# A feed-forward kernel's first microseconds: tile 0 centred by two sums, the bias turned by VectorE, one group of transposes moved

## The chip, the core and the metric

The kernel runs on one core of a Trainium2 chip. The core has five engines that run side by side, each with its own instruction queue: TensorE (PE; its weight loads are listed as PEld), VectorE (DVE), ScalarE (ACT), GpSimd (POOL) and SyncE (SP), which here does nothing but issue DMAs and wait. They wait for each other only where the program says so, on semaphores. The metric is the device time of one execution in microseconds (us), the median of several runs. The core is alone on the chip in these runs.

## The reference

x is 2048 x 1024, w1 is 1024 x 3584, w2 is 3584 x 1024, all bf16. Each row of x is normalized (mean and variance over its 1024 values), multiplied by w1, a bias b1 is added, the approximate GELU is taken, and the result is multiplied by w2 with a bias b2.

```
y = _layernorm(x, axis=-1)
h = _gelu(jnp.einsum("bsd,df->bsf", y, w1) + b1)
return jnp.einsum("bsf,fd->bsd", h, w2) + b2
```

## The kernel before

**Tiling.** The 2048 rows of x are 16 tiles of 128 rows (one row in each partition), and four tiles make a block of 512 rows. For each block the kernel needs the normalized rows transposed (`yT_sb`: the 1024 features in 8 pieces of 128 partitions, 512 rows along), so that the first product gives h transposed (`hT_sb`: 28 rows of 128 hidden features, 512 along). For each of the 28 rows, 8 matmuls of 128x512 add up in one PSUM bank (L416), ACT reads the bank and writes GELU with the bias as a column per partition (L433), and the second product (L467) reads `hT_sb`. There are eight PSUM banks: one for transposes (`ps_t`), five for the first product (`ps_1`), two for the second (`ps_2`).

**The first block.** All data must come from memory, so block 0 starts in small pieces. The first seven hidden rows are computed in a "wave" of cells of 128x128, one cell for each tile, hidden row and feature piece (dt), in an order written out by hand (`order`, L509 to L524). Into it the transposes on PE of tiles 0 to 3 (`pe_T`, L360) are put at fixed places: `T_PUTS` (L24) says after how many cells a group of transposes comes. Tile 0 is transposed in three groups of pieces (`GROUPS_0`: 0-1, 2-4, 5-7), tiles 1 to 3 in two of four. The first two groups of tile 0 come ahead of all cells, the third at place 14. Each group goes to a PSUM bank, and ACT copies it to `yT_sb` (L383); a group that uses the same bank waits for the copy of the group before. Groups 0 and 2 of tile 0 and all groups of tiles 1 to 3 use the bank `ps_t`. From the eighth hidden row on the rows are computed whole, with 128x512 matmuls; each takes a PSUM bank whose GELU must be done.

**Normalizing tile 0.** PE cannot start before something is centred. For tile 0 only the mean is taken first, and the reciprocal deviation is put in later. Before the change the mean is got in two ways at once: ACT sums the left 512 columns (L495), DVE takes the statistics of the right 512 (`bn_stats`, L261, whose output holds the means of even and odd columns), and one small operation on DVE adds the three numbers to four times the mean (`op_mean0`, L272). Then DVE writes 4x - 4m for tile 0 to a spare buffer (L278), in two pieces, columns 0-255 and 256-1023. Tile 1 is also only centred (L283); tiles 2 and 3 are normalized whole (L287), for which POOL raises the variance to the power -1/2 (L265). For tiles 0 and 1 the factor is applied after the first product: DVE spreads the reciprocal deviations of the 256 rows over all partitions (`ops_rbc`: L322 and sixteen 32x32 transposes, L330) and multiplies each accumulated bank by them (`dve_scale`, L426) before GELU. The factor of tile 0 is 0.25 of its reciprocal deviation there, since 4x - 4m was written.

**Bias.** b1 is loaded as 28 rows of 128 (`b1r_sb`), but GELU needs it as 28 columns of one value per partition. PE transposes it together with tile 2's second group (`with_b1`, L365 to L369, `B1_AT`), into the same bank, and ACT casts it to `b1_sb` (L387). Every GELU waits for that.

**Warm-up.** Ahead of real work PE runs matmuls on constants (L491): 34 without a wait, then 3 that wait for tile 0's mean (`WARM_A`, L21), and 3 after tile 0's second group.

**Queues.** SP issues most loads in the order of `SP_FIRST_LOADS` (L33): tile 0's left half, six chunks of w1 (one feature piece for seven hidden rows each, 224 KB), tile 2's halves, b1, two more chunks, tile 3's halves, then w8, a chunk of 1 MB for the next hidden rows; the rest of w1, block 1 of x, w2, b2 and the other blocks follow. ACT issues tile 0's right half and tile 1. DVE's order in the head is a list (`head`, L500), followed by the spreading of the deviations. After the first wave DVE's work is laid out by a planner (L571 to L586) that mixes work with due times (scaling, output) with filling work (normalizing and transposing the next block).

Of the kernel before, what the change touches and what calls it, by code (L numbers as in the profile page):

```python
# [17 lines left out]
NB2 = 2  # L18
NOB = 2
TAIL_PIECES = 4  # L20
WARM_A = ((34, None), (3, "m4"))  # L21
WARM_B = 3
N_CENTRED = 2
T_PUTS = {0: (None, None, 14), 1: (21, 35), 2: (96, 118), 3: (140, 156)}  # L24
NORM = {0: (0, 2, 8), 1: (0, 4, 8), 2: (0, 4, 8)}
GROUPS_0 = (0, 2, 5, 8)
WAVE_ROWS_0 = 6
WAVE_K = (0, 2, 4, 5, 6, 8)
B1_AT = (2, 1)
GROUPS_1 = (0, 4, 8)  # L30
W1_CHUNK_COLS = (512, 512, 1024, 640)
N_W2_CHUNKS = 4
SP_FIRST_LOADS = ("x0a", "w0", "w1", "w2", "w3", "w4", "w5", "x2a", "x2b", "b1", "w6", "w7", "x3a", "x3b", "w8")  # L33
ACT_FIRST_LOADS = ("x0b", "x1")

T_PE_START = 5.7
# [55 lines left out]
def bass_standalone__mixer_channel_mlp__prompt_kernel(  # L92
# [53 lines left out]
    with ExitStack() as es:  # L146
# [7 lines left out]
        hT_sb = sb("hT_sb", [P, FT, TB], BF16)  # L154
        o_sb = sb("o_sb", [P, NOB, D], BF16)
        b2_sb = sb("b2_sb", [P, D], BF16)
        b1r_sb = sb("b1r_sb", [FT, P], BF16)
        b1_sb = sb("b1_sb", [P, FT], F32)
        ident = sb("ident", [P, P], BF16)
        ones = sb("ones", [P, P], BF16)  # L160
# [1 line left out]
        st_sb = sb("st_sb", [P, NT, 15], F32)  # L162
        mv_sb = sb("mv_sb", [P, NT, 2], F32)
        rstd_sb = sb("rstd_sb", [P, NT], F32)
        half_sb = sb("half_sb", [P, 1], F32)
        m4_sb = sb("m4_sb", [P, 1], F32)
        rq_sb = sb("rq_sb", [P, N_CENTRED, 32], F32)
        rbc_sb = sb("rbc_sb", [P, N_CENTRED, P], F32)

# [16 lines left out]
        x_ev = {}  # L186
        w1_issued = set()

        def dma(dst, src, sig, nbytes):
            dma_q[0].op(lambda e, dst=dst, src=src: e.dma_start(dst, src), sig=sig, sem="d_" + sig, inc=16)  # L190
            dma_bytes[0] += nbytes
            est[sig] = DMA_T0 + dma_bytes[0] / DMA_BYTES_PER_US

# [19 lines left out]
        def issue(item):  # L213
            if item[0] == "x" and item[-1] in "ab":
                i, h = int(item[1:-1]), "ab".index(item[-1])
                dma(x_sb[:, i, h * HC:(h + 1) * HC], xf[i * P:(i + 1) * P, h * HC:(h + 1) * HC], f"x{i}_{h}",
                    P * HC * 2)
                x_ev[i] = (f"x{i}_0", f"x{i}_1")
            elif item == "b1":
                dma(b1r_sb[:, :], b1.rearrange("(t p) -> t p", p=P), "b1", F * 2)  # L220
            elif item[0] == "x":
                load_x_tile(int(item[1:]))
            elif item[0] == "w" and int(item[1:]) < len(w1_chunks):
                load_w1(int(item[1:]))
# [7 lines left out]
        for i in range(TPB):  # L232
            if i not in x_ev:
                load_x_tile(i)
            else:
                for h, evn in enumerate(x_ev[i]):
                    if evn not in est:
                        issue(f"x{i}" + "ab"[h])
        if "b1" not in est:
            issue("b1")  # L240
        for ci in range(len(w1_chunks)):
            if ci not in w1_issued:
# [11 lines left out]
                                          compare_op=ALU.is_equal, fill=0.0, base=0, channel_multiplier=1),  # L254
                waits=["ones"], sig="ident")
        pool.op(lambda e: e.memset(nhalf[:, :], -0.5), sig="nhalf")
        pool.op(lambda e: e.memset(st_sb[:, :, 12:14], 0.0))
        pool.op(lambda e: e.memset(st_sb[:, :, 14:15], LN_EPS * D), sig="eps")

        def op_stats(i, h):  # L260
            return (lambda e, i=i, h=h: e.bn_stats(st_sb[:, i, 6 * h:6 * (h + 1)], x_sb[:, i, h * HC:(h + 1) * HC]),  # L261
# [7 lines left out]
                    [f"st{i}_0", f"st{i}_1", "eps"], f"mv{i}", 0.33)  # L269

        def op_mean0():
            return (lambda e: e.tensor_scalar(out=m4_sb[:, :], in0=st_sb[:, 0, 7:8], scalar1=st_sb[:, 0, 10:11],  # L272
                                              scalar2=half_sb[:, :], op0=ALU.add, op1=ALU.add),
                    ["st0_1", "half"], "m4", 0.1)

        def op_norm(i, c0, c1, sig):
            if i == 0:
                return (lambda e, c0=c0, c1=c1: e.tensor_scalar(  # L278
                            out=o_sb[:, 0, c0:c1], in0=x_sb[:, 0, c0:c1], scalar1=4.0,
                            scalar2=m4_sb[:, :], op0=ALU.mult, op1=ALU.subtract),  # L280
                        ["m4"], sig, 0.02 + (c1 - c0) * 0.00055)
            if i < N_CENTRED:
                return (lambda e, i=i, c0=c0, c1=c1: e.tensor_scalar(  # L283
                            out=x_sb[:, i, c0:c1], in0=x_sb[:, i, c0:c1], scalar1=mv_sb[:, i, 0:1],
                            scalar2=None, op0=ALU.subtract),
                        [f"mv{i}"], sig, 0.02 + (c1 - c0) * 0.00055)
            return (lambda e, i=i, c0=c0, c1=c1: e.tensor_scalar(  # L287
                        out=x_sb[:, i, c0:c1], in0=x_sb[:, i, c0:c1], scalar1=mv_sb[:, i, 0:1],
                        scalar2=rstd_sb[:, i:i + 1], op0=ALU.subtract, op1=ALU.mult),
                    [f"rstd{i}", f"mv{i}"], sig, 0.02 + (c1 - c0) * 0.00055)  # L290
# [12 lines left out]
        def ln_seq(tiles, between):  # L303
# [12 lines left out]
                    seq += ops_norm(i)  # L316
            return seq

        def ops_rbc():
            res = []  # L320
            for i in range(N_CENTRED):
                res.append((lambda e, i=i: e.tensor_scalar(out=rq_sb[:, i, :], in0=ones[:, 0:32],  # L322
                                                           scalar1=rstd_sb[:, i:i + 1], scalar2=(1.0 if i else 0.25),
                                                           op0=ALU.mult, op1=ALU.mult),
                            ["ones", f"rstd{i}"], f"rq{i}", 0.1))
            for tq in range(4):
                for q in range(4):
                    src = rq_sb[32 * tq:32 * (tq + 1), :, :]
                    dst = rbc_sb[32 * q:32 * (q + 1), :, 32 * tq:32 * (tq + 1)]
                    res.append((lambda e, src=src, dst=dst: e.transpose(out=dst, in_=src), [f"rq{N_CENTRED - 1}"],  # L330
                                ("rbc" if tq == 3 and q == 3 else None), 0.1))
            return res
# [24 lines left out]
        bank_read = {}  # L357
        t_banks = [("t", ps_t[:, 0, :]), ("2_0", ps_2b[:, 0, :]), ("t", ps_t[:, 0, :])]

        def pe_T(i, groups, k, with_b1=False):  # L360
            blk, t = divmod(i, TPB)
            j0, j1 = groups[k], groups[k + 1]
            bname, bap = t_banks[k if i == 0 else 0]
            evs = yT_ev.setdefault(i, [None] * DT)
            if with_b1:  # L365
                o = (j1 - j0) * P
                b1t = bap[:, o:o + FT]
                pe.op(lambda e: e.transpose(out=b1t, in_=b1r_sb[:, :], identity=ident[0:FT, 0:FT]),  # L368
                      waits=["ident", "b1"] + ([bank_read[bname]] if bname in bank_read else []))  # L369
            for j in range(j0, j1):  # L370
                waits = []
                if j == j0:
                    waits = ["ident"] + ([bank_read[bname]] if bname in bank_read else [])
                if j == j0 or y_ev[i][j] != y_ev[i][j - 1]:
                    waits.append(y_ev[i][j])
                pe.op(lambda e, i=i, j=j, o=(j - j0) * P, bap=bap: e.transpose(  # L376
                    out=bap[:, o:o + P], in_=(x_sb[:, i] if i else o_sb[:, 0])[:, j * P:(j + 1) * P],
                    identity=ident[:, :]),
                    waits=waits, sig=(f"tp{i}_{k}" if j == j1 - 1 else None))
                evs[j] = f"te{i}_{k}"  # L380
            src = bap[:, 0:(j1 - j0) * P].rearrange("p (j s) -> p j s", j=j1 - j0)
            dst = yT_sb[:, blk % 2, j0:j1, t * P:(t + 1) * P]
            act.op(lambda e, dst=dst, src=src: e.copy(out=dst, in_=src), waits=[f"tp{i}_{k}"], sig=f"te{i}_{k}")  # L383
            bank_read[bname] = f"te{i}_{k}"
            if with_b1:
                bank_read[bname] = "b1c"
                act.op(lambda e: e.copy(out=b1_sb[:, :], in_=b1t), waits=[f"tp{i}_{k}"], sig="b1c")  # L387
            pe_t[0] += (j1 - j0) * 0.056

        crit = []  # L390
# [98 lines left out]
        def warm(n, gate=None):  # L489
            for _ in range(n):  # L490
# [1 line left out]
                                         start=True, stop=True), waits=[gate] if gate else [])  # L492

        act.op(lambda e: e.preload_act_table(ACT.Gelu_apprx_tanh))
        act.op(lambda e: e.activation(out=o_sb[:, 1, 0:HC], in_=x_sb[:, 0, 0:HC], func=ACT.Copy, scale=2.0 / HC,  # L495
                                      accum_out=half_sb[:, :]), waits=[x_ev[0][0]], sig="half")
        for n, gate in WARM_A:
            warm(n, gate)
        dve.op(None, waits=["eps"])
        head = [op_stats(0, 1), op_mean0()] + ops_norm(0) + ln_seq([1], ()) + [op_stats(0, 0), op_aggr(0)]  # L500
        for o in head + ln_seq(list(range(2, TPB)), ()) + ops_rbc():
            dve_put(o)

        for k in range(2):
# [19 lines left out]
            order.insert(n, ("T", t, k))  # L524
        for c in order:
            if c[0] == "T":
                pe_T(c[1], GROUPS_1 if c[1] else GROUPS_0, c[2], with_b1=(c[1:] == B1_AT))
# [102 lines left out]
```

## Time and profile before

| | us |
|---|---|
| median of 3 runs (398.64 to 398.94) | 398.64 |
| the profiled execution | 398.81 |
| its span | 397.5 |
| PE busy | 394.0 |
| DVE busy | 152.8 |
| ACT busy | 83.0 |
| first cell of the wave starts | 5.98 |
| tile 1's first transposes start | 7.66 |
| first matmul of the eighth hidden row starts | 20.64 |

All times of the profile count from the start of the span. Duration and idle time are given for each instruction or group; "idle before" names what ended the wait. The chain that ended last follows the work backward from the end, from each instruction to what released it. A matmul's shown duration (0.22 us for 128 columns) includes its way through the array; matmuls overlap, and in a full stretch of the wave they start 0.056 us apart (61 cells in 3.41 us of the chain).

### The profile page before, as it was taken

The page shows a single profiled execution, that of the slowest core. Times are in us where ns is not written, and L with a number is a line of the kernel's source. Part 1 is how long each engine was busy: PE and PEld are TensorE (multiplying, and loading weights), DVE is VectorE, ACT ScalarE, POOL GpSimd, SP SyncE. Part 2 cuts the span into 40 slices and gives each one's busy share as a digit, 9 for nine tenths or more (in the row PEclk, how much of TensorE's full clock was granted, in tenths as well). Part 3 has the DMA queues.
Part 4 walks back from the last instruction along what each step waited for, and adds up shares of the span by engine and source line. Part 5 has one row for each costly group of instructions (what it writes and reads, how often), then busy time and mean ns, then how long its engine had stood idle before and what let it go on. Part 6 is the DMA issues. An engine that isn't in the chain of part 4 may idle for free.

```text
span 397.5 us, 4880 instructions
## 1 busy us (share of the span) xinstructions
PE 394.0 (99%) x2117; PEld 191.4 (48%) x2117; DVE 152.8 (38%) x341; ACT 83.0 (21%) x125; POOL 9.8 (2%) x25
## 2 busy tenths in 40 slices
PE   8999999999999999999999999999999999999998
PEld 7954444444444444444444444444444444444447
DVE  5837899989999005988100000001100000001011
ACT  4364330000134432000024434100003334400000
POOL 2101000020001000000000000000000000000000
DMA  8999930000000000000000000000000000000000
GB/s 288 359 378 386 387 136 13 26 29 13 27 2 0 2 0 0 29 13 26 28 13 0 2 0 2 11 16 28 13 26 15 0 0 2 0 13 28 13 28 26
DMA packets 16798, 23.64 MB, mean 59 GB/s; under 512 B 1546, under 2 KB 10378, under 8 KB 16778
## 3 DMA queue, kind: packets, MB, share of 16 engines
q1 hardware_dynamic: 16490, 22.95, 16.4%
q10 hardware_dynamic: 288, 0.39, 0.3%
q8 instruction: 16, 0.26, 0.3%
q14 instruction: 4, 0.03, 0.0%
HBM read 19.14 MB, written 4.19 MB: 59 GB/s over the span
## 4 chain that ended last, share of the span: by engine, by line
PE 98%; DMA 1%; DVE 0%; ACT 0%; issue 0%; DVEq 0%
PE ps L467 49%; PE ps L416 41%; PE ps_t L416 8%; DMA x_sb<-in_x_dram 1%; PE ps_t L376 1%; DVE st_sb L261 0%; PE ps L491 0%; ACT yT_sb L383 0%; PE ps L376 0%; DVE o_sb L478 0%; DVE m_sb L272 0%; PE ps_t L368 0%; DVEq L79 0%
## 5 line engine op out<-in xcount | busy, mean ns | idle before, releaser
L467 PE MATMUL ps<-w_sb,hT_sb 128*128 128x512 bf16 (+1 forms) x980 | 194.2, 361 | 0.0
L416 PE MATMUL ps<-yT_sb,w_sb 128*128 128x512 bf16 (+1 forms) x920 | 167.3, 340 | 0.1
L467 PEld LDWEIGHTS ps<-w_sb,hT_sb 128*128 128x128 bf16 x980 | 91.3, 98 | 102.6
L416 PEld LDWEIGHTS ps<-yT_sb,w_sb 128*128 128x128 bf16 x920 | 80.9, 98 | 82.3 <-issue 0.2
L433 ACT ACTIVATE hT_sb<-ps,b_sb 128x512 bf16<-128x512 f32 x94 | 63.9, 688 | 236.6 <-PE ps L416 217.1
L478 DVE TENSOR_TENSOR o_sb<-ps,b_sb 128x512 bf16<-128x512 f32 (+1 forms) x35 | 22.6, 646 | 198.2 <-PE ps L467 198.1
L348 DVE STREAM_TRANSPOSE yT_sb<-x_sb 32x256 bf16<-32x256 bf16 x192 | 83.7, 436 | 26.6 <-PE ps_t L416 23.5
L416 PE MATMUL ps_t<-yT_sb,w_sb 128*128 128x512 bf16 x144 | 34.0, 379 | 0.0
L261 DVE BATCH_NORM_STATS2 st_sb<-x_sb 128x6 f32<-128x512 bf16 x32 | 21.1, 673 | 4.3 <-DMA x_sb<-in_x_dram 4.2
L416 PEld LDWEIGHTS ps_t<-yT_sb,w_sb 128*128 128x128 bf16 x144 | 14.1, 98 | 16.7
L433 ACT ACTIVATE hT_sb<-ps_t,b_sb 128x512 bf16<-128x512 f32 x18 | 12.4, 689 | 17.4 <-PE ps_t L416 14.5
L426 DVE TENSOR_TENSOR ps<-ps,rbc_sb 128x256 f32<-128x256 f32 x24 | 9.7, 428 | 7.0 <-PE ps L416 6.7
L265 POOL TENSOR_TENSOR rstd_sb<-mv_sb,nhalf 128x1 f32<-128x1 f32 x16 | 8.9, 559 | 119.2 <-DVE mv_sb L268 119.2
L287 DVE TENSOR_SCALAR x_sb<-x_sb,mv_sb,rstd_sb 128x1024 bf16<-128x1024 bf16 (+1 forms) x15 | 7.8, 525 | 3.9 <-POOL rstd_sb L265 3.3
L383 ACT COPY yT_sb<-ps_t 128x512 bf16<-128x512 bf16 (+2 forms) x8 | 4.4, 545 | 8.6 <-PE ps_t L376 8.6
L491 PE MATMUL ps<-const-bfloat16-1.0 128*128 128x128 bf16 x40 | 4.0, 278 | 1.4 <-PEq L615 0.8
L491 PEld LDWEIGHTS ps<-const-bfloat16-1.0 128*128 128x128 bf16 x40 | 3.6, 129 | 1.5 <-issue 0.8
L268 DVE BATCH_NORM_AGGREGATE mv_sb<-st_sb 128x2 f32<-128x15 f32 x16 | 3.5, 221 | 1.3
L330 DVE STREAM_TRANSPOSE rbc_sb<-rq_sb 32x64 f32<-32x64 f32 x16 | 3.8, 236 | 0.2
L376 PE MATMUL ps_t<-ident,x_sb 128*128 128x128 bf16 x24 | 2.4, 220 | 0.2 <-ACT yT_sb L383 0.2
L426 DVE TENSOR_TENSOR ps_t<-ps_t,rbc_sb 128x256 f32<-128x256 f32 x4 | 1.6, 410 | 1.7 <-PE ps_t L416 1.7
L376 PEld LDWEIGHTS ps_t<-ident,x_sb 128*128 128x128 bf16 x24 | 1.5, 98 | 0.4 <-ACT yT_sb L383 0.4
(24 smaller groups left out, 7.6 us busy)
## 6 DMA issues: line engine op xcount, KB each, us to landing
w_sb<-in_w_dram SPq DMA_DIRECT2D x4, 1792.0 KB, 18.1
out_dram<-o_sb SPq DMA_DIRECT2D x31, 128.0 KB, 1.7
x_sb<-in_x_dram SPq DMA_DIRECT2D x3, 1024.0 KB, 14.0
w_sb<-in_w_dram SPq DMA_DIRECT2D x2, 1024.0 KB, 9.6
w_sb<-in_w_dram SPq DMA_DIRECT2D x1, 2048.0 KB, 15.1
w_sb<-in_w_dram SPq DMA_DIRECT2D x8, 224.0 KB, 4.2
w_sb<-in_w_dram SPq DMA_DIRECT2D x1, 1280.0 KB, 15.4
x_sb<-in_x_dram SPq DMA_DIRECT2D x5, 128.0 KB, 4.2
```

The lines of the kernel that those rows point to most:

```text
L261: return (lambda e, i=i, h=h: e.bn_stats(st_sb[:, i, 6 * h:6 * (h + 1)], x_sb[:, i, h * HC:(h + 1) * HC]), [x_ev[i][h]], f"st{i}_{h}", 0.65)
L265: pool.op(lambda e, i=i: e.tensor_tensor(out=rstd_sb[:, i:i + 1], in0=mv_sb[:, i, 1:2], in1=nhalf[:, i:i + 1], op=ALU.pow), waits=[f"mv{i} ...
L287: return (lambda e, i=i, c0=c0, c1=c1: e.tensor_scalar(out=x_sb[:, i, c0:c1], in0=x_sb[:, i, c0:c1], scalar1=mv_sb[:, i, 0:1], scalar2=rst ...
L348: res.append((lambda e, src=src, dst=dst: e.transpose(out=dst, in_=src), waits, (f"tr{i}" if lastop else None), 0.47))
L376: pe.op(lambda e, i=i, j=j, o=(j - j0) * P, bap=bap: e.transpose(out=bap[:, o:o + P], in_=(x_sb[:, i] if i else o_sb[:, 0])[:, j * P:(j + ...
L383: act.op(lambda e, dst=dst, src=src: e.copy(out=dst, in_=src), waits=[f"tp{i}_{k}"], sig=f"te{i}_{k}")
L416: pe.op(lambda e, b=b, r=r, dt=dt, n0=n0, n1=n1, bank=bank: e.matmul(unit_bank(bank)[:, n0:n1], lhsT=w1_sb[:, dt, r * P:(r + 1) * P], rhs= ...
L426: crit.append((est[wait_ev], (lambda e, ap=ap: e.tensor_tensor(out=ap, in0=ap, in1=rbc_sb[:, :, :].rearrange("p t s -> p (t s)"), op=ALU.m ...
L433: act.op(lambda e, r=r, n0=n0, n1=n1, bank=bank: e.activation(out=hT_sb[:, r, n0:n1], in_=unit_bank(bank)[:, n0:n1], func=ACT.Gelu_apprx_tanh,
L467: pe.op(lambda e, st=st, ft=ft, c0=c0, c1=c1, bank=bank: e.matmul(ps_2[:, bank, 0:c1 - c0], lhsT=hT_sb[:, ft, st * P:(st + 1) * P], rhs=w2 ...
L478: crit.append((est[sig], (lambda e, ob=ob, c0=c0, c1=c1, bank=bank: e.tensor_tensor(out=o_sb[:, ob, c0:c1], in0=ps_2[:, bank, 0:c1 - c0], ...
L491: pe.op(lambda e: e.matmul(ps_1[:, 0, 0:P], lhsT=unit, rhs=unit, start=True, stop=True), waits=[gate] if gate else [])
```

## The change

Six things are edited together.

1. Tile 0's sums: ACT sums the right half scaled by 1/1024 (event `mean_1`), DVE the left half with a `tensor_scalar` that also gives a sum (event `mean_0`). Each sum is one column of `m_sb`. Nothing adds them: the centring subtracts one column and then the other, and writes x - m instead of 4x - 4m. The factor 0.25 is gone.
2. Tile 0's statistics, formerly the first of DVE's work (right half) and behind tile 1 (left half and aggregate), come behind tile 2's aggregate (left half) and behind tile 3's (right half and aggregate).
3. The bias: four loads of 28 rows of 32 values go to the four groups of 32 partitions of a zeroed buffer, one DVE transpose in 32x32 blocks turns all four, and a DVE copy casts to fp32. These two come on DVE after the head and ahead of the spreading of the deviations. The transpose on PE and the cast on ACT are gone. The loads come behind tile 3's halves instead of ahead of the seventh chunk of w1, and each waits for the zeroing.
4. The third group of tile 0's transposes comes after 6 cells instead of 14.
5. Warm-up: 32 matmuls instead of 34, then 2 instead of 3, which wait for ACT's sum.
6. Two small memsets move from POOL to DVE, and POOL gets the zeroing of the bias buffer.

```diff
-WARM_A = ((34, None), (3, "m4"))
+WARM_A = ((32, None), (2, "mean_1"))
-T_PUTS = {0: (None, None, 14), 1: (21, 35), 2: (96, 118), 3: (140, 156)}
+T_PUTS = {0: (None, None, 6), 1: (21, 35), 2: (96, 118), 3: (140, 156)}
-B1_AT = (2, 1)
-SP_FIRST_LOADS = ("x0a", "w0", "w1", "w2", "w3", "w4", "w5", "x2a", "x2b", "b1", "w6", "w7", "x3a", "x3b", "w8")
+SP_FIRST_LOADS = ("x0a", "w0", "w1", "w2", "w3", "w4", "w5", "x2a", "x2b", "w6", "w7", "x3a", "x3b", "b1", "w8")
...
-                dma(b1r_sb[:, :], b1.rearrange("(t p) -> t p", p=P), "b1", F * 2)
+                b1v = b1.rearrange("(t q a) -> q t a", q=4, a=32)
+                for q in range(4):
+                    dma(b1r_sb[32 * q:32 * q + FT, :], b1v[q], f"b1{q}", F // 2, waits=["b1z"])
...
-        pool.op(lambda e: e.memset(st_sb[:, :, 12:14], 0.0))
-        pool.op(lambda e: e.memset(st_sb[:, :, 14:15], LN_EPS * D), sig="eps")
+        pool.op(lambda e: e.memset(b1r_sb[:, :], 0.0), sig="b1z")
+        dve.op(lambda e: e.memset(st_sb[:, :, 12:14], 0.0))
+        dve.op(lambda e: e.memset(st_sb[:, :, 14:15], LN_EPS * D), sig="eps")
...
         def op_mean0():
-            return (lambda e: e.tensor_scalar(out=m4_sb[:, :], in0=st_sb[:, 0, 7:8], scalar1=st_sb[:, 0, 10:11],
-                                              scalar2=half_sb[:, :], op0=ALU.add, op1=ALU.add),
-                    ["st0_1", "half"], "m4", 0.1)
+            return (lambda e: e.tensor_scalar(out=o_sb[:, 1, HC:D], in0=x_sb[:, 0, 0:HC], scalar1=1.0 / D, scalar2=None,
+                                              op0=ALU.mult, op1=ALU.add, accum_out=m_sb[:, 0:1]),
+                    [x_ev[0][0]], "mean_0", 0.7)
...
-                            out=o_sb[:, 0, c0:c1], in0=x_sb[:, 0, c0:c1], scalar1=4.0,
-                            scalar2=m4_sb[:, :], op0=ALU.mult, op1=ALU.subtract),
-                        ["m4"], sig, 0.02 + (c1 - c0) * 0.00055)
+                            out=o_sb[:, 0, c0:c1], in0=x_sb[:, 0, c0:c1], scalar1=m_sb[:, 0:1],
+                            scalar2=m_sb[:, 1:2], op0=ALU.subtract, op1=ALU.subtract),
+                        ["mean_0", "mean_1"], sig, 0.02 + (c1 - c0) * 0.00055)
...
+        def ops_b1():
+            return [(lambda e: e.transpose(out=b1t_sb[:, :], in_=b1r_sb[:, :]), [f"b1{q}" for q in range(4)], "b1t", 0.2),
+                    (lambda e: e.tensor_copy(b1_sb[:, :], b1t_sb[:, 0:FT]), ["b1t"], "b1c", 0.1)]
...
-        act.op(lambda e: e.activation(out=o_sb[:, 1, 0:HC], in_=x_sb[:, 0, 0:HC], func=ACT.Copy, scale=2.0 / HC,
-                                      accum_out=half_sb[:, :]), waits=[x_ev[0][0]], sig="half")
+        act.op(lambda e: e.activation(out=o_sb[:, 1, 0:HC], in_=x_sb[:, 0, HC:D], func=ACT.Copy, scale=1.0 / D,
+                                      accum_out=m_sb[:, 1:2]), waits=[x_ev[0][1]], sig="mean_1")
...
-        dve.op(None, waits=["eps"])
-        head = [op_stats(0, 1), op_mean0()] + ops_norm(0) + ln_seq([1], ()) + [op_stats(0, 0), op_aggr(0)]
-        for o in head + ln_seq(list(range(2, TPB)), ()) + ops_rbc():
+        head = [op_mean0()] + ops_norm(0) + ln_seq([1], ())
+        mid = {2: lambda: [op_stats(0, 0)], 3: lambda: [op_stats(0, 1), op_aggr(0)]}
+        for i in range(2, TPB):
+            head += [op_stats(i, 0), op_stats(i, 1), op_aggr(i)] + mid[i]() + ops_norm(i)
+        for o in head + ops_b1() + ops_rbc():
             dve_put(o)
```

In `pe_T` the lines under `with_b1` (L365 to L369 and L385 to L387) are taken out.

More of the change, by code (lines that the diff above doesn't have):

```diff
@@ L156, in bass_standalone__mixer_channel_mlp__prompt_kernel @@
         b2_sb = sb("b2_sb", [P, D], BF16)
-        b1r_sb = sb("b1r_sb", [FT, P], BF16)
+        b1r_sb = sb("b1r_sb", [P, 32], BF16)
+        b1t_sb = sb("b1t_sb", [P, 32], BF16)
         b1_sb = sb("b1_sb", [P, FT], F32)
@@ L164, in bass_standalone__mixer_channel_mlp__prompt_kernel @@
         rstd_sb = sb("rstd_sb", [P, NT], F32)
-        half_sb = sb("half_sb", [P, 1], F32)
-        m4_sb = sb("m4_sb", [P, 1], F32)
+        m_sb = sb("m_sb", [P, 2], F32)
         rq_sb = sb("rq_sb", [P, N_CENTRED, 32], F32)
@@ L187, in bass_standalone__mixer_channel_mlp__prompt_kernel, with dma @@
         w1_issued = set()
-        def dma(dst, src, sig, nbytes):
-            dma_q[0].op(lambda e, dst=dst, src=src: e.dma_start(dst, src), sig=sig, sem="d_" + sig, inc=16)
+        def dma(dst, src, sig, nbytes, waits=()):
+            dma_q[0].op(lambda e, dst=dst, src=src: e.dma_start(dst, src), waits=waits, sig=sig, sem="d_" + sig, inc=16)
             dma_bytes[0] += nbytes
@@ L238, in bass_standalone__mixer_channel_mlp__prompt_kernel @@
                         issue(f"x{i}" + "ab"[h])
-        if "b1" not in est:
+        if "b10" not in est:
             issue("b1")
@@ L322, in ops_rbc @@
                 res.append((lambda e, i=i: e.tensor_scalar(out=rq_sb[:, i, :], in0=ones[:, 0:32],
-                                                           scalar1=rstd_sb[:, i:i + 1], scalar2=(1.0 if i else 0.25),
-                                                           op0=ALU.mult, op1=ALU.mult),
+                                                           scalar1=rstd_sb[:, i:i + 1], scalar2=None, op0=ALU.mult),
                             ["ones", f"rstd{i}"], f"rq{i}", 0.1))
@@ L358, in bass_standalone__mixer_channel_mlp__prompt_kernel, with pe_T @@
         t_banks = [("t", ps_t[:, 0, :]), ("2_0", ps_2b[:, 0, :]), ("t", ps_t[:, 0, :])]
-        def pe_T(i, groups, k, with_b1=False):
+        def pe_T(i, groups, k):
             blk, t = divmod(i, TPB)
@@ L364, in pe_T @@
             evs = yT_ev.setdefault(i, [None] * DT)
[L365 to L369, printed above, removed]
             for j in range(j0, j1):
@@ L384, in pe_T @@
             bank_read[bname] = f"te{i}_{k}"
-            if with_b1:
-                bank_read[bname] = "b1c"
-                act.op(lambda e: e.copy(out=b1_sb[:, :], in_=b1t), waits=[f"tp{i}_{k}"], sig="b1c")
             pe_t[0] += (j1 - j0) * 0.056
@@ L526, in bass_standalone__mixer_channel_mlp__prompt_kernel @@
             if c[0] == "T":
-                pe_T(c[1], GROUPS_1 if c[1] else GROUPS_0, c[2], with_b1=(c[1:] == B1_AT))
+                pe_T(c[1], GROUPS_1 if c[1] else GROUPS_0, c[2])
             else:
```

## The prediction

> **What bounds the kernel now.** I read the totals first, then the chain that ended last, then the first 23 us of the timeline, then the landing times of the loads there.
>
> ```profile
> PE 394.0 (99%) x2117; PEld 191.4 (48%) x2117; DVE 152.8 (38%) x341; ACT 83.0 (21%) x125; POOL 9.8 (2%) x25
> ...
> PE 98%; DMA 1%; DVE 0%; ACT 0%; issue 0%; DVEq 0%
> ```
>
> TensorE (PE) is the bound, and the chain leaves it only at the start. So this change can give only what PE still waits for, or does needlessly, in the head. The chain in order of time shows that part:
>
> ```profile
> 0.78 2.80 DMA x_sb<-in_x_dram
> ...
> 6.92 0.18 PE ps_t L376 x3
> 7.10 0.02 issue
> 7.13 0.49 ACT yT_sb L383
> 7.61 0.05 issue
> 7.66 0.40 PE ps_t L376 x4
> ...
> 13.99 0.12 PE ps_t L368
> ```
>
> There are three places: from the landing of tile 0's right half (0.78 + 2.80 = 3.58) to the first transpose; the stay on ACT at 7.13, where PE waits for a copy of tile 0's third group; and the bias transpose (L368). From 7.66 to the end PE has no gap of over 0.1 us but the one at L368. The timeline gives the lines that price the change:
>
> ```profile
> 3.43 0.63 ACT L495 ACTIVATE o_sb<-x_sb 128x512 bf16<-128x512 bf16 x1 [0.45 <-DMA x_sb<-in_x_dram]
> 3.96 0.19 ACT L495 ACTIVATION_READ_ACCUMULATOR o_sb<-x_sb 128x1 f32 x1
> 4.72 0.29 DVE L278 TENSOR_SCALAR o_sb<-x_sb,m_sb 128x256 bf16<-128x256 bf16 x1
> 4.92 0.41 DVE L278 TENSOR_SCALAR o_sb<-x_sb,m_sb 128x768 bf16<-128x768 bf16 x1
> 5.25 0.69 DVE L261 BATCH_NORM_STATS2 st_sb<-x_sb 128x6 f32<-128x512 bf16 x1
> 5.98 0.94 PE L416 MATMUL ps<-yT_sb,w_sb 128*128 128x128 bf16 x14
> 6.89 0.35 DVE L283 TENSOR_SCALAR x_sb<-x_sb,mv_sb 128x512 bf16<-128x512 bf16 x1
> 11.11 0.41 DVE L287 TENSOR_SCALAR x_sb<-x_sb,mv_sb,rstd_sb 128x512 bf16<-128x512 bf16 x1
> 14.57 3.98 DVE L330 STREAM_TRANSPOSE rbc_sb<-rq_sb 32x64 f32<-32x64 f32 x16
> 18.83 2.44 DVE L426 TENSOR_TENSOR ps<-ps,rbc_sb 128x256 f32<-128x256 f32 x7 [0.27 <-PE ps L416]
> ```
>
> Columns are start, duration, engine and line; in brackets the idle time before.
>
> **Step 1, the centre of tile 0.** Before, by the same chain, DVE takes statistics of the right half (3.68 to 4.38), combines them (4.41 to 4.69) and subtracts from 4.72. Now ACT sums the right half while DVE sums the left. ACT's pair took 3.43 to 4.15, 0.72. Started at 3.68, where DVE got the right half, it ends at 4.40; a handover cost 0.04 to 0.06 in the rows (ACT to PE 7.61 to 7.66), so the subtraction starts at 4.45, not 4.72. DVE's sum has no row. The nearest are a 512-wide subtraction without a sum (0.35) and one 512-wide statistics pass plus a one-column operation (0.69 + 0.27 = 0.96); from 3.43 it ends between 3.78 and 4.39, hidden by ACT's 4.40 at both ends. Without that cover (a sum of 1.2 us) the excess of 0.2 would eat most of the gain. The subtraction now reads two columns instead of one: L287 with two took 0.41 for 512 columns, L283 with one 0.35, so 0.06 more for each of two pieces. The first piece ends at 4.45 + 0.29 + 0.06 = 4.80 instead of 5.01: 0.21 sooner. The second starts 0.26 after the first and takes 0.47, so it ends at 5.18 instead of 5.33. Transposes, copy and the first cell follow the first piece: 5.98 becomes 5.77. Bounds: 0.28 if ACT wakes 0.04 after the landing as it did for the left half; 0.05 if ACT loses 0.16 to anything.
>
> **Step 2, the third group sooner.** PE's seven cells before tile 1's first transposes start at 6.93 and end at 6.93 + 7 x 0.056 = 7.32; the transposes start at 7.66. So 0.34 is a wait for the third group's copy. With that group after 6 cells instead of 14, it starts at 5.77 + 6 x 0.056 = 6.10; from first transpose to free bank took 0.90 (6.76 to 7.66), so the copy is done at 7.00. PE arrives at 7.32 - 0.21 = 7.11: that wait is gone. Late next is tile 1's normalization. Its first statistics start at 5.25 now; its load (ACT's second, issued at about 1.24, 3.9 us to landing) comes in at 5.1 to 5.2, so they cannot move by the full 0.15. I take 5.20. From there to the end of the first L283 piece is 6.89 + 0.35 - 5.25 = 1.99, so 7.19, and 0.06 to PE: 7.25. Steps 1 and 2 together bring 7.66 to 7.25, 0.41. Bounds: 0.36 (statistics not sooner than 5.25) and 0.55 (PE's own 7.11). A weight chunk could be late instead:
>
> ```profile
> w_sb<-in_w_dram SPq DMA_DIRECT2D x2, 224.0 KB, 4.3
> x_sb<-in_x_dram SPq DMA_DIRECT2D x1, 128.0 KB, 4.4
> ```
>
> (the loads by issue, the first line in the stretch 3.0 to 3.3, the second in 4.0 to 4.2). The fifth chunk is issued at about 3.1 and lands at 7.4 to 7.5; its first cell now starts at 7.25 + 0.22 + 0.39 = 7.86. It is covered by about 0.4.
>
> **Step 3, the bias off PE.** 22 cells from 12.60 end at 13.82, and the next transposes of x start at 14.04; at the two like places (12.38, 15.50) the gap is 0.02. So the bias transpose costs PE 0.20, and all of it is on the path. Low bound 0.12, what the chain books on it. ACT's cast (0.19) goes too, beside PE.
>
> **Step 4, what DVE does instead.** Tile 2's first half is issued at 4.06 and lands 4.4 later, 8.46, right before its statistics at 8.50. So taking tile 0's left statistics and aggregate (0.92 between 7.42 and 8.37) out from ahead of them gains nothing. The left statistics now fill the 0.66 in which DVE waited for POOL before 10.78, so tile 2 ends as before. The right ones and the aggregate (0.69 + 0.22) stand in the like gap before 13.70 and push tile 3's normalization by about 0.17, to 14.42. Its transposes are due at 15.50 - 0.61 = 14.89: covered by 0.4. Then come a 32-column transpose and a copy for the bias, nearest rows 0.24 (L330) and 0.19 (ACT's cast), then the 16 broadcasts as before, which end near 19.1 instead of 18.55. The first scaling starts near 19.15 instead of 18.83, its GELU ends near 20.3, and the row on PE that needs that bank starts at 22.36 - 0.61 = 21.75. Cover 1.4, so I cost it at nothing. POOL's power for tile 0 now comes behind tile 3's, at about 14.0 to 14.6; the broadcasts need it, and the bias's two operations fill that wait.
>
> **Step 5, the queues.** On SP one bias load (0.46 of issue) leaves the place ahead of two weight chunks and tile 3's halves, which go out 0.46 sooner, and four of about 0.45 stand ahead of the 1 MB chunk, which goes out about 1.3 later, at 8.7. It is first needed at 20; it now lands near 14. All later loads move by at most that, and DVE needs block 1's data (first used at 30.37) for matmuls at 105. The four loads each wait for POOL's zeroing, which comes where the memsets of the statistics were (1.3 to 1.5), long before SP arrives. They land near 8.3 + 4.4 = 12.7; DVE wants them at 14.4, and the broadcasts queue behind that wait. Cost nothing, cover 1.7 and behind it the 1.4 of step 4. The memsets move to DVE, idle until 3.4.
>
> **Step 6, fewer warm-up matmuls.** 32 instead of 34 end 0.11 sooner, then PE waits as before; two gated ones instead of three start at 4.45 and are over before 4.8. No cost on the path, unless the clock suffers (below).
>
> **The sum.** 0.41 + 0.20 = 0.61. The profiled execution took 398.81 (span 397.5 and 1.3 around it), so 398.2 for it. It stands 0.17 above the median of the three runs, so the median becomes 398.03, say 398.0: -0.15%. I call a difference real from 0.2% (0.8 us), about what this kernel's measurement can tell; the three runs differ by 0.3.
>
> **Rivals.**
> Smaller gain: DVE's sum or ACT's start is late, and PE meets tile 1 at 7.30 or later. Then 0.15 to 0.45 remains, 398.2 to 398.5. For it: tile 1's load lands where DVE wants it. Against it: the bias's 0.20 is independent.
> Larger gain: ACT wakes at 3.62, tile 1's load is in time, nothing stalls before 7.66. 0.28 + 0.34 + 0.22 = 0.84, 397.8. Against it: the 3.9 us landing.
> Slower, by the bias wait on DVE: the four small loads land late, and the scaling behind them holds PE's banks. From landing to the end of the first GELU is about 6.0 us (bias 0.4, broadcasts 4.4, scaling and GELU 1.2), so landings after 15.7 cost PE their whole excess, and after 17.1 the kernel is over 0.8 slower: 399.5 at 17.1. For it: the old single load shows no landing time. Against it: its neighbours on SP land in 4.0 to 4.5.
> Slower, by the clock: in the head PE begins about 12 warm-up matmuls in each us from 1 to 3, 16 from 3 to 4, and 22 per us later, so it comes to full rate near 3.5. With fewer matmuls and a wait behind them the half rate could return or last. Each matmul would then cost 0.05 more; it takes 28 of the 57 between 5.77 and 8.9 to turn 0.61 faster into 0.8 slower (399.4), and all 57 give 2.9 - 0.6 slower, 400.9. Against it: the wait shrinks from 0.56 to about 0.4. The Trainium skill, "TensorE: Matmul & The Clock Gate", Part 1, says that full rate is granted after about 3.4 us of a busy window that runs on its own phase, and lost after an idle window of that length. The trace has full rate 2.7 us after PE's first matmul, which fits such a phase; by that rule a wait of 0.4 loses nothing, and only a late phase would hurt.
>
> **How the numbers follow.** As summed, 0.45 to 0.75 gained (397.9 to 398.2): 0.55. Smaller gain: 0.16. Larger: 0.15. Bias wait: 0.06. Clock: 0.08. Faster by over 0.2% is the larger gain, 0.15; slower the last two, 0.14; within is 0.71. From the 0.15 faster I keep the near half, and from the slower cases none beyond 399: range 397.5 to 398.9.
>
> **What would show it.** Step 1: the subtraction near 4.45 and the first cell near 5.77. Step 2: no wait on ACT before tile 1's transposes, which start near 7.25. Step 3: no PE gap near 13.4. Steps 4 and 5: bias loads landed before 14, tile 3 normalized before 14.9, PE never waiting for ACT after 20. Step 6: matmuls 0.056 apart from the first cell. It is wrong if DVE's sum takes over 1 us, if a load lands late, or if early cells run at half rate.

## The result and the profile after

The changed kernel takes 398.38 us (median of 21 executions, 398.02 to 399.21), the kernel before, run beside it, 398.99 (398.64 to 399.63). The ratio is 0.9986, with a 95% interval of 0.998 to 0.9992: 0.61 us faster, small but outside its uncertainty. The interval of the gain is about 0.32 to 0.80 us. The prediction was a gain of 0.61 and a median of 398.0. The gain came out, closer than a measurement of this width can confirm; the level is 0.38 higher, because the forecast started from three runs of before whose median, 398.64, lies 0.35 under that of the 21 runs.

The first two lines are the totals and the chain's shares of the changed kernel's profile, which answer to those shown of before. PE's work has shrunk by the bias transpose and the warm-up, and nothing else has become the bound.

```profile
PE 393.7 (99%) x2113; PEld 191.2 (48%) x2113; DVE 153.5 (39%) x346; ACT 82.9 (21%) x124; POOL 9.9 (2%) x24
...
PE 98%; DMA 1%; ACT 0%; DVE 0%; issue 0%; DVEq 0%
```

The chain of the changed kernel in order of time (start, duration, what), over the stretch in which before had its three stops:

```profile
0.78 3.03 DMA x_sb<-in_x_dram
...
3.83 0.73 ACT o_sb L492 x2
...
4.67 0.36 DVE o_sb L280
...
5.99 0.49 PE ps L413 x6
6.49 0.17 PE ps_t L376 x3
6.65 0.84 PE ps L413 x15
7.49 0.36 PE ps_t L376 x4
...
12.55 1.23 PE ps L413 x22
13.78 0.22 PE ps_t L376 x4
```

The stay on ACT ahead of tile 1's transposes is gone, and so is the bias transpose between the 22 cells and tile 2's second group. The first cell, though, starts at 5.99, where before had 5.98. The reason is in the first line: here tile 0's right half landed at 0.78 + 3.03 = 3.81, in the trace of before at 3.58. Measured from the landing, the first cell comes after 2.18 instead of 2.40.

Lines from the timeline of the changed kernel (start, duration, engine, line; idle time before in brackets; other lines are left out):

```profile
3.64 0.69 DVE L274 TENSOR_SCALAR_CACHE_REDUCE o_sb<-x_sb 128x512 bf16<-128x512 bf16 x1 [2.66 <-DMA x_sb<-in_x_dram]
4.25 0.08 DVE L274 DVE_READ_ACCUMULATOR o_sb<-x_sb 128x1 f32 x1
4.67 0.74 DVE L280 TENSOR_SCALAR o_sb<-x_sb,m_sb 128x256 bf16<-128x256 bf16 x2 [0.34 <-ACT o_sb L492]
5.33 1.28 DVE L263 BATCH_NORM_STATS2 st_sb<-x_sb 128x6 f32<-128x512 bf16 x2
6.96 0.62 DVE L285 TENSOR_SCALAR x_sb<-x_sb,mv_sb 128x512 bf16<-128x512 bf16 x2
7.47 0.38 PE L376 MATMUL ps_t<-ident,x_sb 128*128 128x128 bf16 x4
8.64 1.29 DVE L263 BATCH_NORM_STATS2 st_sb<-x_sb 128x6 f32<-128x512 bf16 x2 [1.06 <-DMA x_sb<-in_x_dram]
14.31 0.20 DVE L322 STREAM_TRANSPOSE b1t_sb<-b1r_sb 128x32 bf16<-128x32 bf16 x1
15.25 3.98 DVE L335 STREAM_TRANSPOSE rbc_sb<-rq_sb 32x64 f32<-32x64 f32 x16
19.34 2.42 DVE L423 TENSOR_TENSOR ps<-ps,rbc_sb 128x256 f32<-128x256 f32 x7
```

DVE's sum (0.69 with the read of its result) is over at 4.33, 0.23 before ACT's (4.56). Tile 1's transposes start at 7.47, 0.14 behind where PE's own work would have put them. DVE takes the bias at 14.31 without a wait. The scaling starts at 19.34, and PE starts the eighth row at 20.21 and the next at 21.93 without a wait.

### The profile page after: what moved, and what is told of

Same layout as the page of the kernel before. It is cut to its first block, busy times and chain, and to the rows that moved or that the text cites. A ratio compares the mean times of both kernels' runs of the same rounds, so it can differ in the third digit from the quotient of the medians.

```text
span 397.1 us, 4877 instructions
## 1 busy us (share of the span) xinstructions
PE 393.7 (99%) x2113; PEld 191.2 (48%) x2113; DVE 153.5 (39%) x346; ACT 82.9 (21%) x124; POOL 9.9 (2%) x24
## 4 chain that ended last, share of the span: by engine, by line
PE 98%; DMA 1%; ACT 0%; DVE 0%; issue 0%; DVEq 0%
PE ps L464 49%; PE ps L413 41%; PE ps_t L413 8%; DMA x_sb<-in_x_dram 1%; PE ps_t L376 0%; ACT o_sb L492 0%; DVE o_sb L280 0%; PE ps L376 0%; DVE o_sb L475 0%; PE ps L488 0%; DVEq L78 0%
```

## The experiments

Each was timed beside the kernel before. Differences below are of medians, against the kernel before that was timed beside it; for a group of 11 executions the interval of a ratio is about 0.0009 to each side (0.35 us), so single steps of 0.2 us are read in the traces, and the times only support them.

**The group alone.** On the kernel before, one number:

```diff
-T_PUTS = {0: (None, None, 14), 1: (21, 35), 2: (96, 118), 3: (140, 156)}
+T_PUTS = {0: (None, None, 6), 1: (21, 35), 2: (96, 118), 3: (140, 156)}
```

> The kernel before, with only the third group of tile 0's transposes after 6 cells instead of 14. Measured inside the profile, from the landing of tile 0's right half to the first matmul of the eighth hidden row, which was 20.64 - 3.58 = 17.06 us before and is 20.21 - 3.81 = 16.40 after the whole change. Theory (three gains that add up, of 0.21 by the sums, 0.21 by the group, 0.21 by the bias): the wait for the third group's copy goes, and tile 1's normalization, done at 3.66 after the landing with about 0.12 to PE, becomes the next limit: tile 1's transposes at 3.78 instead of 4.08, so 16.76, and about 0.3 us off the time; more than its share in the whole change, because the sums' gain overlaps with it. Rival (the group's place pays nothing without the earlier centre, tile 1 was about to be late anyway): 17.06, time unchanged.

Measured: 0.28 us less, ratio 0.9992 (0.9984 to 1.0001). In the timeline of this kernel:

```profile
4.56 0.62 DVE L278 TENSOR_SCALAR o_sb<-x_sb,m_sb 128x256 bf16<-128x256 bf16 x2
5.26 1.29 DVE L261 BATCH_NORM_STATS2 st_sb<-x_sb 128x6 f32<-128x512 bf16 x2
5.82 0.50 PE L416 MATMUL ps<-yT_sb,w_sb 128*128 128x128 bf16 x6
7.41 0.38 PE L376 MATMUL ps_t<-ident,x_sb 128*128 128x128 bf16 x4
```

The time agrees with the expected 0.3, the expected marks do not: tile 1's transposes come 3.99 after the landing (at 3.42), not 3.78, and PE's wait ahead of them is still 0.25 (7.41 less 5.82 and the 1.335 of work between). So this trace shows only 0.09 gained (3.99 against 4.08), and the 0.28 of the times, whose interval includes no gain, is not explained by it. The centring ends at 5.18, so DVE could have begun tile 1's statistics at about 5.10, as it overlaps its instructions by 0.08 elsewhere (in the changed kernel the centring ends at 5.41 and the statistics start at 5.33). It began at 5.26: tile 1's load was the limit. A measure from the landing of tile 0's right half alone is wrong for this, since two loads that land independently decide.

What holds better is the distance from the start of tile 1's statistics to its transposes on PE. In the traces of this kernel, the changed kernel (twice) and three variants of it told below (statistics in front, old warm-up, halves swapped), which all have the third group after 6 cells, it is 2.14 or 2.15 (5.26 to 7.41 here, 5.33 to 7.47 in the changed kernel). With the group after 14 it is 2.41 in the kernel before, 2.35 with the sums alone and 2.25 in the changed kernel with the group put back. So the group's move does take the copy's wait away, and tile 1's normalization is the next limit, as forecast; but what sets it is now DVE, now the load.

**The bias alone.** On the kernel before, the four loads, the zeroing, `ops_b1` behind the head, and no bias on PE or ACT:

```diff
...
-        for o in head + ln_seq(list(range(2, TPB)), ()) + ops_rbc():
+        for o in head + ln_seq(list(range(2, TPB)), ()) + ops_b1() + ops_rbc():
...
```

> The kernel before, with only the bias turned by DVE (four loads, zeroed buffer, transpose and copy on DVE, nothing on PE and ACT). Theory: the gap of 0.20 on PE ahead of tile 2's second transposes goes, landing to eighth row 16.86, time 0.2 us less. Rival (the four small loads and the two DVE operations ahead of the broadcasts give it back as a wait of DVE, or of PE after 20 us): 17.06 or more, with a PE wait on ACT or DVE after the eighth row.

Measured: 0.18 us less, ratio 0.9996 (0.9987 to 1.0004). From the 22 cells to tile 2's second transposes it takes 1.23 (13.15 to 14.38) instead of 1.44 (12.60 to 14.04), and there is no wait after the eighth row: 0.21, as expected. The expected sum from the landing could not be read, because in this trace PE stopped for weights:

```profile
7.67 0.56 PE L415 MATMUL ps<-yT_sb,w_sb 128*128 128x128 bf16 x7 [0.51 <-DMA w_sb<-in_w_dram]
```

The third chunk took 5.48 us to land, from its issue at 2.15. Nothing ahead of that load differs from the kernel before, where it took 4.1.

**The sums alone.** On the kernel before, the two sums with the later statistics, all else as before:

```diff
...
-        head = [op_stats(0, 1), op_mean0()] + ops_norm(0) + ln_seq([1], ()) + [op_stats(0, 0), op_aggr(0)]
+        head = [op_mean0()] + ops_norm(0) + ln_seq([1], ())
...
```

> The kernel before, with only the two sums and the later statistics of tile 0 (group after 14 cells, bias on PE, 34 and 3 warm-up matmuls as before). Theory: from the landing to the first cell 2.40 becomes 2.18, and the wait for the third group's copy moves with it and stays as long: tile 1's transposes at 3.87 instead of 4.08, eighth row 16.85, time 0.2 us less. Rival (the gain of the whole change sits in the group and the bias, and the sums are given back at tile 1): first cell sooner but eighth row at 17.06, time unchanged.

Measured: 0.16 us less, ratio 0.9998 (0.9989 to 1.0007). The first cell comes 2.17 after the landing at 3.66 instead of 2.40, and the wait for the third group's copy goes along unchanged: from the first cell to tile 1's transposes it takes 1.68 (5.83 to 7.51), as before (5.98 to 7.66). The three parts alone gave 0.28, 0.18 and 0.16 us, 0.62 together; the whole change gave 0.61. With 0.35 to each side for every part, this agreement is luck; what the parts are worth is read from the traces.

**The change without the group.** The changed kernel with the third group back at 14:

> The changed kernel with the third group back after 14 cells. Theory: the wait of about 0.34 for its copy is back, tile 1's transposes at 3.87 after the landing instead of 3.66, eighth row 16.61, time 0.2 us more than the changed kernel and 0.4 less than the kernel before. Rival (tile 1's normalization is the limit either way): 16.40, time as with the whole change.

Measured: 0.36 less than before, ratio 0.9993 (0.9984 to 1.0002), and so 0.25 more than the whole change against the kernel before timed beside that. The landing was at 3.60, the first cell at 5.78 (2.18), tile 1's transposes at 7.46 (3.86, expected 3.87). The wait is back: once the sums are in, the group is worth 0.20 in the traces (3.86 less 3.66).

**Tile 0's statistics back in front.** The changed kernel with these statistics ahead of tile 2's, by

```diff
+        head = [op_mean0()] + ops_norm(0) + ln_seq([1], ()) + [op_stats(0, 0), op_stats(0, 1), op_aggr(0)]
+        head += ln_seq(list(range(2, TPB)), ())
```

in place of the loop that spreads them:

> The changed kernel with tile 0's statistics and aggregate ahead of tile 2's statistics instead of in the gaps behind tile 2's and tile 3's aggregate. Theory (the statistics' place is free, because DVE waits 1.06 us there for tile 2's load and has 0.3 us or more to PE behind): they take 1.55 from 7.55, tile 2's statistics start near 9.1 instead of 8.64, its normalization is done near 11.8 for transposes due at 12.17, tile 3's near 14.8 for 15.07; no wait on PE, time as with the whole change within 0.1 us. Rival (the later statistics carry part of the 0.6): PE waits at 12.17 or 15.07, time 0.2 to 0.6 us more.

Measured: 0.72 less than before, ratio 0.9982 (0.9974 to 0.9991), no slower than the change. Tile 3's normalization ends at 14.58 for transposes at 14.95, and PE waits neither for tile 2 nor for tile 3. That the statistics come later still, in the gaps behind tile 2 and tile 3, is worth nothing; what the sums need is only that they no longer stand ahead of the centring.

**The warm-up of before.** The changed kernel with

```diff
-WARM_A = ((32, None), (2, "mean_1"))
+WARM_A = ((34, None), (3, "mean_1"))
```

> The changed kernel with the warm-up of before, 34 and then 3 matmuls. Theory (the two or three fewer cost nothing: PE came to full rate at 3.55 to 4.8 us in eight of the nine traces with 32 or 34, whichever it was): same time as the changed kernel within 0.1 us, three gated matmuls over before the first transpose. Rival (fewer warm-up matmuls make late full rates as in one trace, 6.64 us, more frequent): 0.1 to 0.3 us less than the changed kernel, and fewer slow runs at the upper end.

Measured: 0.53 less than before, ratio 0.9987 (0.9978 to 0.9995); the changed kernel beside it 0.65 less, ratio 0.9988 (0.9979 to 0.9997). No gain from more warm-up matmuls.

> The changed kernel once more, unedited, on the chip and in the call of the next three, as their measure. Theory (three gains of about 0.2): 0.6 us less than the kernel before. Rival (part of the first 0.61 was the spread of loads and clock between runs): 0.4 or less.

That second measurement of the whole change, 0.65, agrees with the first, 0.61.

**Half the warm-up.** The changed kernel with 16 instead of 32:

> The changed kernel with 16 warm-up matmuls instead of 32 ahead of the two that wait. Theory (32 instead of 34 costs nothing because PE comes to full rate at about 3.5 while the warm-up still runs, and the following wait of under 0.5 does not lose it; but the full rate does need the work before it): here the warm-up ends near 2.5, the rate is not raised at 3.5, and the first cells start 0.107 apart; time 0.8 to 2.9 us more. Rival (the rate comes without that work, or the second group of three and the transposes are enough): cells 0.056 apart from the first, time unchanged.

Measured: 0.58 us more than the kernel before, ratio 1.0017 (1.0008 to 1.0026), so about 1.2 more than the changed kernel. Stretches of 1 us of its trace, with PE's busy time behind the comma, its matmuls in the bracket after that, and the granted clock third from the end:

```profile
6.00:7.00 1.00, 1.00 (x13) 1.00 (x11) 0.86 (x3) 0.30 (x1) 0.16 (x1) 1.00 1.03 385
7.00:8.00 1.00, 1.00 (x12) 1.00 (x11) 0.40 (x2) 0.48 (x1) 0.56 (x1) 1.00 0.99 338
8.00:9.00 1.00, 1.00 (x13) 1.00 (x11) 0.24 (x1) 0.00 (x0) 0.00 (x0) 1.00 1.08 391
...
10.00:11.00 1.00, 1.00 (x22) 1.00 (x19) 0.82 (x3) 0.58 (x1) 0.55 (x1) 1.00 0.95 226
```

and the same stretch of the changed kernel:

```profile
6.00:7.00 1.00, 1.00 (x19) 1.00 (x20) 0.86 (x4) 0.63 (x2) 0.00 (x0) 1.00 1.03 391
```

Until 8.9 us the matmuls start 0.107 apart, half the rate, and the granted clock reads 1.00 all the same: here the rate is seen in the number of matmuls alone. So the clock rival's mechanism exists and its price is real. The median with 32 matmuls doesn't pay it, the one with 16 does; but single executions with 32 come to full rate late too, as told below.

**The halves swapped.** The changed kernel with ACT on the left half and DVE on the right:

```diff
-            return (lambda e: e.tensor_scalar(out=o_sb[:, 1, HC:D], in0=x_sb[:, 0, 0:HC], scalar1=1.0 / D, scalar2=None,
+            return (lambda e: e.tensor_scalar(out=o_sb[:, 1, HC:D], in0=x_sb[:, 0, HC:D], scalar1=1.0 / D, scalar2=None,
...
-        act.op(lambda e: e.activation(out=o_sb[:, 1, 0:HC], in_=x_sb[:, 0, HC:D], func=ACT.Copy, scale=1.0 / D,
-                                      accum_out=m_sb[:, 1:2]), waits=[x_ev[0][1]], sig="mean_1")
+        act.op(lambda e: e.activation(out=o_sb[:, 1, 0:HC], in_=x_sb[:, 0, 0:HC], func=ACT.Copy, scale=1.0 / D,
+                                      accum_out=m_sb[:, 1:2]), waits=[x_ev[0][0]], sig="mean_1")
```

> The changed kernel with the halves swapped: ACT sums the left half, which has landed about 0.2 us sooner in all traces so far, DVE the right one. Theory (the centre waits for the sum of the late half and its way to DVE: on ACT 0.73 and 0.11, on DVE 0.69 and no handover): the subtraction starts about 0.75 after the landing of the right half instead of 0.86, the first cell 2.08 instead of 2.18 after it, time 0.1 us less than the changed kernel where tile 1 does not limit, 0 where it does. Rival (which engine sums the late half is indifferent, the two loads land together often enough): unchanged.

Measured: 0.74 less than before, ratio 0.9984 (0.9975 to 0.9993).

```profile
3.80 0.69 DVE L274 TENSOR_SCALAR_CACHE_REDUCE o_sb<-x_sb 128x512 bf16<-128x512 bf16 x1 [2.81 <-DMA x_sb<-in_x_dram]
4.41 0.08 DVE L274 DVE_READ_ACCUMULATOR o_sb<-x_sb 128x1 f32 x1
4.53 0.73 DVE L280 TENSOR_SCALAR o_sb<-x_sb,m_sb 128x256 bf16<-128x256 bf16 x2
```

The subtraction starts 0.73 after the start of the late sum, where it took 0.84 on ACT (3.83 to 4.67). The first cell comes 2.08 after the landing (3.77 to 5.85), as expected. So the mechanism is shown in the trace; the 0.1 is inside the spread of the times.

**Cells ahead of tile 1.** The changed kernel with

```diff
-T_PUTS = {0: (None, None, 6), 1: (21, 35), 2: (96, 118), 3: (140, 156)}
-WAVE_K = (0, 2, 4, 5, 6, 8)
+T_PUTS = {0: (None, None, 6), 1: (24, 42), 2: (96, 118), 3: (140, 156)}
+WAVE_K = (0, 2, 4, 6, 6, 8)
```

> The changed kernel with tile 1's first transposes after 24 cells instead of 21, tile 0's cells of the sixth feature piece ahead of tile 1's cells, and tile 1's second transposes after 42 cells instead of 35. Theory (after the change PE's one wait left is 0.15 for tile 1's normalization, and 0.03 for its copy): from the first cell to tile 1's first transposes no gap over 0.02, eighth row 0.15 to 0.2 sooner, time 0.15 us less than the changed kernel. Rival (weights come next: the sixth chunk, issued at 3.6, lands 8.1 to 8.5 or later and its cells would start near 8.3): PE waits there for the load, nothing gained or up to 0.5 us lost, with a wider spread between runs.

Measured: 0.78 less than before, ratio 0.9985 (0.9976 to 0.9994); the 0.17 beyond the changed kernel's 0.61 is inside the uncertainty. PE has no wait at tile 1:

```profile
5.73 0.53 PE L488 MATMUL ps<-const-bfloat16-1.0 128*128 128x128 bf16 x3
6.06 0.76 PE L413 MATMUL ps<-yT_sb,w_sb 128*128 128x128 bf16 x6
6.66 0.33 PE L376 MATMUL ps_t<-ident,o_sb 128*128 128x128 bf16 x3
6.82 1.17 PE L413 MATMUL ps<-yT_sb,w_sb 128*128 128x128 bf16 x18
7.83 0.39 PE L376 MATMUL ps_t<-ident,x_sb 128*128 128x128 bf16 x4
```

The 18 cells end at 6.82 + 18 x 0.056 = 7.83, where the transposes start. But this execution also shows something else. The first six cells take from 6.06 to 6.66, 0.1 apart, and only then come 0.056 apart: PE's full rate came at 6.6, with the same 32 warm-up matmuls. So the trace can't be compared place by place with the changed kernel's, and it does not show that a wait was saved.

**Both together.**

> The changed kernel with both the halves swapped and tile 1's transposes after 24 and 42 cells. Theory (each takes its own wait: 0.1 at the centre, 0.15 to 0.2 at tile 1): no PE gap over 0.03 between the first cell and 12 us, eighth row 0.25 sooner than in the changed kernel with like loads, time 0.85 us less than before. Rival (the two waits are the same wait on the loads, seen in two places): time as with one of them alone.

Measured: 0.71 less than before (0.65 for the changed kernel beside it), ratio 0.9981 (0.9972 to 0.9990). It has the lowest single time of all (397.95), but its interval covers that of the changed kernel, so it isn't shown to beat it. The expected lack of gaps did not come. Its chain:

```profile
3.58 4.98 DMA w_sb<-in_w_dram
8.56 0.05 issue
8.61 0.56 PE ps L413 x7
```

The sixth chunk landed at 8.56, and its cells, moved ahead of tile 1's, waited 0.2 for it. It is not the only stop in this trace: cells at 7.17 waited about 0.1 for the fourth chunk, and tile 1's transposes at 7.54 about 0.2 for DVE, whose statistics of tile 1 had waited for the load and started at 5.39. The time is that of one of the two edits alone, as the rival said. The rival of the run before is right too: behind tile 1 the weights stand.

**Tile 1's load in two.** The changed kernel with

```diff
-ACT_FIRST_LOADS = ("x0b", "x1")
+ACT_FIRST_LOADS = ("x0b", "x1a", "x1b")
```

> The changed kernel with tile 1's load in two halves on ACT's queue. Theory (in the traces where the right half of tile 0 landed early, tile 1's statistics began at 5.2 to 5.26 whatever DVE did before, so its load is the limit there): its first half lands before 5.1, the statistics begin right behind the centring, tile 1's transposes up to 0.1 sooner, time 0 to 0.1 us less. Rival (DVE is the limit, the load is in time): statistics where they were, time unchanged or, by ACT's additional issue ahead of its sum, up to 0.1 more.

Measured: only 0.13 less than before, ratio 0.9994 (0.9985 to 1.0002), so 0.5 worse than the changed kernel: neither of the two.

```profile
5.18 0.69 DVE L263 BATCH_NORM_STATS2 st_sb<-x_sb 128x6 f32<-128x512 bf16 x1
6.40 0.69 DVE L263 BATCH_NORM_STATS2 st_sb<-x_sb 128x6 f32<-128x512 bf16 x1 [0.53 <-DMA x_sb<-in_x_dram]
7.96 0.38 PE L376 MATMUL ps_t<-ident,x_sb 128*128 128x128 bf16 x4 [0.43 <-DVE x_sb L285]
```

The first half was in time, the second landed at 6.38, a full microsecond after the whole load does. The later load passes straight through to PE's wait, which confirms that tile 1's load stands right behind the group's copy. Why the second half lands so late was not tried. The trace has one sign: it was issued at 1.70, the whole load at 1.21, and it landed 0.31 behind the chunk of w1 that SP issued at 1.69, while the whole load landed ahead of that chunk in every trace.

## Why the prediction was right

Step 1, the centre: forecast 0.21 sooner for the first cell, measured 0.22 from the landing in the trace after and in the one without the group. Inside it two terms were off and cancelled, by luck. ACT began its sum 0.02 after the landing, not 0.10, and the way from ACT to DVE took 0.11 (4.56 to 4.67), not 0.05. DVE's sum, without a row before, took 0.69, between the bounds of 0.35 and 0.96, and lay hidden as forecast.

The 0.22 holds only where PE is at full rate by then. In the second trace of the changed kernel it was not: the first cell comes 2.28 after the landing at 0.78 + 2.76 = 3.54, a gain of 0.12, as also in the other traces in which full rate came after 5.5 us (2.28 or 2.29). Lines of that second trace:

```profile
0.78 2.76 DMA x_sb<-in_x_dram
```

```profile
5.49 0.42 PE L488 MATMUL ps<-const-bfloat16-1.0 128*128 128x128 bf16 x3
5.82 0.49 PE L413 MATMUL ps<-yT_sb,w_sb 128*128 128x128 bf16 x6
7.19 0.38 PE L376 MATMUL ps_t<-ident,x_sb 128*128 128x128 bf16 x4
```

It cost nothing there: tile 1's transposes start 3.65 after the landing, against 3.66 in the first trace, since in both they wait for DVE.

Step 2, the group: forecast a wait of 0.14 left for tile 1's normalization, measured 0.14 (6.49 + 15 x 0.056 = 7.33 to 7.47). From the landing to tile 1's transposes it takes 3.66, before 4.08: 0.42, forecast 0.41. That tile 1's normalization comes next was right; that the number came out to 0.01 was luck again, for two terms cancel. The forecast had tile 1's statistics wait for the load until 5.20, 1.62 after the landing; they started at 5.33, 1.52 after it, right behind the centring and with no wait for the load. And the way from DVE to PE, for which the forecast took 0.06 from a row of ACT, takes 0.14 (5.03 to 5.17 in the chain after; before, 5.01 to 5.16 already). The group alone showed that the load, which the forecast took for the bound, is the limit in some executions.

Step 3, the bias: forecast 0.20, measured 0.21 (12.39 to 13.62, before 12.60 to 14.04).

Step 4, DVE: tile 3 normalized at 14.39, forecast 14.42; broadcasts over at 19.23, forecast 19.1; first scaling at 19.34, forecast 19.15; no wait of PE behind it. Step 5: the 1 MB chunk issued at 8.66, forecast 8.7. Step 6: nothing, and nothing with 34 and 3.

The smaller gain is there, as an execution: with the old warm-up, where tile 1's load came at 5.32, PE's wait at tile 1 was 0.43, and the transposes start 4.04 after the landing, almost as late as before. The larger gain is not. PE's wait was only 0.04 in the second trace of the changed kernel (5.82 to 7.19), but because PE itself came 0.10 later. The bias wait did not come. The clock rival was wrong in its cause, the two matmuls fewer, but full rate near 3.5 was wrong too, as something to rely on. Step 6's sign, cells 0.056 apart from the first, failed with the cells ahead of tile 1 and with the split load. The late phase of which the forecast spoke is there: see below.

One sentence on measurement was too cautious. I took 0.2% as about what can be told from no change; with 21 executions on each side 0.14% was told.

## What to carry to other kernels

When one engine is busy for 99%, list its waits one by one, ask for each what is late next, and cost the change by that next thing; here each of three small edits took away its own stop, and what it was worth was set by the next one. A sum that comes out to 0.01 can still hold terms that are each off by 0.1. Compare marks from the event that the edit depends on, and check that only one such event decides: a load that lands 0.2 us later hides a gain of 0.2. An order of work made tighter on one input (tile 1's copy) soon leans on the next ones (tile 1's load, then the weights), and those vary from one execution to the next.

## What the runs showed of the hardware

When PE comes to full rate differs between executions of the same opening work. By the distance of the matmuls' starts, 0.107 before and 0.056 after, it came at 3.55 in the trace of before, 3.76 in that of the change, at about 4.2 with the group alone, 5.55 with the old warm-up, 5.7 in the second trace of the change, 6.1 with the split load and 6.6 with the cells ahead; with 16 warm-up matmuls at 8.9. In the other six traces it fell into PE's waits between 4.1 and 5.2. The Trainium skill, "TensorE: Matmul & The Clock Gate", Part 1, says that the window of about 3.4 us in which activity is judged runs freely and is not reset by the kernel, so that the moment varies, by 0.5 us to each side. The traces agree that it varies, but by more than that: 3.1 us among kernels that run 32 or 34 warm-up matmuls, about one such window. Where it came after 5.5 us, the first cell was 0.1 later; at 6.6 it cost about 0.05 more on each of six cells. That it makes part of the spread between executions (398.02 to 399.21 for the changed kernel) is likely but was not measured, since only one timed execution of each kernel has a trace.

The other part that the traces show is the loads: tile 0's right half landed between 3.42 and 3.81, and the third chunk once after 5.48 us, with the same instructions ahead of them.
